# Clearing the buffer of the experts' results: one memset on GpSimd, or eight copies on ScalarE

## The chip, the cores and the metric

The kernel runs on one core of a Trainium2 chip. The metric is device time in microseconds (us) of one execution, as the median of three runs. Engines are called by short names: PE is TensorE (its matmuls; PEld its weight loads), ACT is ScalarE, DVE is VectorE, POOL is GpSimd, SP is the engine that issues most DMAs. Each engine works through its own list of instructions in order; an instruction that waits holds up everything behind it on that engine.

## The reference

Three stages follow each other on 2304 tokens (4 batches of 576).

```python
kv = einsum('bhsd,bhse->bhde', k, v); out = einsum('bhsd,bhde->bhse', q, kv)
x = out / sqrt(mean(out*out) + 1e-6) * g_norm            # attention, 8 heads of 64

logits = x @ w_gate                                      # 8 experts, top 1
e = argmax(logits); gate = softmax(logits)[e]; pos = rank of the token within its expert
h = relu(disp[e] @ w1[e]); y = h @ w2[e]                 # 512 -> 1024 -> 512
out[i] = gate * y[e, pos]                                # if pos < capacity, else 0

a = x @ moe2_w1; b = x @ moe2_w2                         # bilinear stage
out = ((a * b) @ w3) @ w_out
```

## The kernel before, in words

The attention stage takes about the first 75 us; it ends with the gate: for each expert the rows that chose it. The **expert stage** then goes through the eight experts in order of their size (`r` = 0 to 7); expert `r` gets a fixed number of rows `NR[r]` (376, 342, ... 272). Its work is cut into eight steps `m` = 0 to 7, one for each 128 of the 1024 hidden features. In a step PE computes `hp` (`emit_mm1`, L815, 12 matmuls: four pieces of the 512 inputs, three passes each, since every fp32 operand is split into a high part and a low part), ACT writes the high part of `h = relu(hp)` and DVE its low part (`emit_h`, L795 and L799), and two steps later PE multiplies that `h` by the second weight into `yp` (`emit_mm2`, L832, 12 matmuls). So `emit_mm2(r, m - 2)` stands behind `emit_mm1(r, m)` in PE's list, and the low part of h(m-2) must be there by then.

Around these matmuls ACT and DVE have three other jobs in every step, in an order that is written out by hand:

- the expert weights come as pieces of 512 KB (`raw`); ACT writes the high part of a piece (`split_hi`, L731), DVE the low part in two halves (`split_lo`, L740), and then the next piece is loaded
- the weights of the last stage come as 64-bit numbers and are converted in four parts: `conv_a` on ACT (L193, L194), `conv_b` on DVE (L206, L208, L213, L216, L221, L223), `conv_c` on ACT (L239), `conv_d` on DVE (L246). After L213 the next such load is issued; three buffers are in turn
- in steps 4 to 6 the rows of the next expert are transposed (`emit_xt`: PE L764 into `xtp`, ACT L766, DVE L769 and L773); POOL gathered them from DRAM one expert ahead (`emit_gather`, L752) and writes the gates and row numbers to `cmeta` (`emit_meta`, L785)

The results of the experts are copied from PSUM into one buffer in SBUF, `yb` (128 partitions x 4 x 2246 fp32; `emit_y`, L846, L847 and L850, on ACT). Where an expert's columns begin in it is known only at run time, so some columns may not be written by any expert; therefore the whole buffer is cleared once before (L1017, by `POOL.memset`). The first results come into it in step 1 of the second expert.

In the list of POOL the clear stands behind the three gathers of expert 1 and the three `cmeta` writes of expert 0; behind it POOL has nothing before the `cmeta` writes of expert 1. `trir` is a small table of constants whose first row is zeros.

After the experts, nine blocks of 256 rows go through the bilinear stage (L867) and the projection (L884), and the rows are scattered to the output by POOL.

Of the kernel before, what the change touches and what calls it, by code (L numbers as in the profile page):

```python
# [24 lines left out]
def kernel(  # L25
# [39 lines left out]
    PE_, ACT, DVE, POOL, SP = nc.tensor, nc.scalar, nc.vector, nc.gpsimd, nc.sync  # L65
# [5 lines left out]
    YB = sum(NR) - Y0  # L71
    KC = D // 128
# [52 lines left out]
    def ring(name):  # L125
        return ring_p.tile([128, 2, 1024], F32R, tag="ring", name=name)
# [70 lines left out]
    def conv_b():  # L197
        if not stage["b"]:
            return
        c_, raw, x, c = stage["b"].pop(0)  # L200
        if is64:
            TS, STT = DVE.tensor_scalar, DVE.scalar_tensor_tensor
            wh = raw[:, :, 1]
            xi = x.bitcast(I32)
            t = cv_p.tile([128, 512], BF16, tag="t", bufs=1, name="t")
            TS(out=x, in0=x, scalar1=2.0 ** -15, scalar2=122880.0, op0=ALU.max, op1=ALU.min)  # L206
            yield
            TS(  # L208
                out=xi, in0=xi, scalar1=3, scalar2=0x3FFFFFFF,
                op0=ALU.logical_shift_left, op1=ALU.bitwise_and,  # L210
            )
            yield
            STT(out=xi, in0=wh, scalar=-(1 << 30), in1=xi, op0=ALU.bitwise_and, op1=ALU.bitwise_or)  # L213
            load_conv()
            yield
            TS(  # L216
                out=t.bitcast(I16), in0=x.bitcast(I16).rearrange("p (n two) -> p n two", two=2)[:, :, 1],
                scalar1=-128, scalar2=None, op0=ALU.bitwise_and,
            )
            yield  # L220
            DVE.tensor_tensor(out=c, in0=t, in1=c, op=ALU.mult)  # L221
            yield
            DVE.tensor_tensor(out=x, in0=x, in1=c, op=ALU.add)  # L223
        stage["c"].append((c_, x))

    def conv_c():
        if not stage["c"]:
            return
        (what, j, s, _), x = stage["c"].pop(0)
        if what == "u":  # L230
            if is64:
                SP.dma_start(out=ud[j, :, 512 * s:512 * s + 512], in_=x)
            else:
                load_conv()
            return
        if what == "w3" and j not in w3t:
            w3t[j] = ring("w3t")
        t = (wo_t[:, j] if what == "wo" else w3t[j])[:, :, 512 * s:512 * s + 512]
        ACT.copy(t[:, 0], x)  # L239
        stage["d"].append((what, j, x, t))  # L240
# [11 lines left out]
    def weave(*steps):  # L252

        steps = [x for x in steps if x]
        while steps:
            for x in list(steps):
                if next(x, 0) == 0:
                    steps.remove(x)
# [20 lines left out]
    trir = const.tile([128, E, E], F32, name="trir")  # L279
# [445 lines left out]
    def split_hi():  # L725

        i = len(piece)
        if i < NP and raws:
            t = raws.pop(0)
            piece[i] = u7_p.tile([128, 2, 1024], F32R, name="piece") if i == NP - 1 else ring("piece")  # L730
            ACT.copy(piece[i][:, 0, :], t)  # L731
            his.append((piece[i], t))

    def split_lo():

        if his:
            s, t = his.pop(0)
            for h in range(2):
                c = slice(512 * h, 512 * h + 512)
                DVE.tensor_tensor(out=s[:, 1, c], in0=t[:, c], in1=s[:, 0, c].bitcast(F32), op=ALU.subtract)  # L740
                if h == 0:
                    yield
            next_load()
# [14 lines left out]
    def emit_xt(r, j):  # L758
        n = min(128, NR[r] - 128 * j)
        if j == 0:  # L760
            xt[r] = xt_p.tile([128, 2, KC, NR[r]], F32R, tag="xt", name="xt")
        p = one_bank("xtp", [128, KC, 128])
        for c in range(KC):
            PE_.transpose(p[:, c, 0:n], rows[r][0:n, j, 128 * c:128 * c + 128], ident[0:n, 0:n])  # L764
        s = slice(128 * j, 128 * j + n)
        ACT.activation(out=xt[r][:, 0, :, s], in_=p[:, :, 0:n], func=AF.Copy, scale=g2[:, 0:1])  # L766

        def lo():
            DVE.scalar_tensor_tensor(  # L769
                out=xt[r][:, 1, :, s], in0=p[:, :, 0:n], scalar=g2[:, 0:1],  # L770
                in1=xt[r][:, 0, :, s].bitcast(F32), op0=ALU.mult, op1=ALU.subtract,
            )
            DVE.tensor_tensor(  # L773
                out=mt[0:n, r, j, 1:2], in0=rows[r][0:n, j, D:D + 1], in1=keep3[0:n, j:j + 1], op=ALU.mult
            )

        return lo

    def emit_meta(r):
        _, o = nc.values_load_multi_w_load_instructions(  # L780
            rr_i[0:1, 1, r:r + 1], engines=[ET.Pool], min_val=0, max_val=sum(NR[:r])
        )
        for j in range(3):
            n = min(128, NR[r] - 128 * j)
            POOL.dma_start(out=cmeta[ds(o[0] + 128 * j, n), :], in_=mt[0:n, r, j, :])  # L785
# [20 lines left out]
    def emit_mm1(r, m):  # L806
        n = NR[r]
        w = piece[8 * r + 2 * (m // 2)].rearrange("p s (c f) -> p s c f", c=KC)
        p = one_bank("hp")
        i = 0  # L810
        order = [(c, a, b_) for c in range(KC) for a, b_ in PASSES]
        if r == 0 and m == 0:
            order = [(c, a, b_) for a, b_ in PASSES for c in range(KC)]
        for c, a, b_ in order:
            PE_.matmul(  # L815
                p[:, 0:n], lhsT=w[:, a, c, 128 * (m % 2):128 * (m % 2) + 128], rhs=xt[r][:, b_, c, :],
                start=(i == 0), stop=(i == 3 * KC - 1),
            )
            i += 1
        hl[m] = p  # L820
# [128 lines left out]
    with tc.manual_schedule():  # L949
# [48 lines left out]
        yb = y_p.tile([128, KC, YB], F32, name="yb")  # L998
# [15 lines left out]
        rows.pop(0)  # L1014
        emit_gather(1)
        emit_meta(0)
        POOL.memset(yb, 0.0)  # L1017
        split_hi()
        weave(split_lo())
        conv_a()  # L1020
# [4 lines left out]
        for r in range(E):  # L1025
            for m in range(NM):
                i = NM * r + m
                cum += slack[i]
                k = min(len(conv_src), GAP + int((len(conv_src) - GAP) * cum / tot_)) - done
                done += k  # L1030
                ready = [f for f in w3t if w3left[f] == 0]

                xl = None
                if r + 1 < E and m in (4, 5, 6):
                    xl = emit_xt(r + 1, m - 4)
                emit_mm1(r, m)

                bs = [conv_b() for _ in range(min(k, len(stage["b"])))]
                for _ in range(len(stage["c"])):
                    conv_c()  # L1040
                for g in bs:
                    next(g, 0)
                weave(split_lo())
                if xl:
                    xl()
                for g in bs:
                    next(g, 0)
                for _ in range(len(stage["d"])):
                    conv_d()
                for g in bs:  # L1050
                    next(g, 0)
                for f in late:
                    f()
                late = []
                hlo = emit_h(r, m)
                hlo()
                weave(*bs)
                if m >= 2:
                    emit_mm2(r, m - 2)
                elif r:  # L1060
                    emit_mm2(r - 1, NM - 2 + m)
                if m == 1 and r:
                    emit_y(r - 1)
                for f in ready:
                    if f < NG - 1:
                        late.append(emit_w34(f))
                split_hi()
                for _ in range(2 - len(stage["b"])):
                    conv_a()
                if r + 1 < E and m == 7:  # L1070
                    rows.pop(r + 1)
                    emit_meta(r + 1)
                    if r + 2 < E:
                        emit_gather(r + 2)
                if r == E - 1 and m == 3:
                    ACT.copy(ys0[:, 0], yb[:, :, YB - Y0:YB])
                if r == E - 1 and m in (4, 5):
                    c = slice(2 * m - 8, 2 * m - 6)
                    DVE.tensor_tensor(
                        out=ys0[:, 1, c, :], in0=yb[:, c, YB - Y0:YB], in1=ys0[:, 0, c, :].bitcast(F32),  # L1080
                        op=ALU.subtract,
                    )
# [213 lines left out]
```

## Time and profile before

| | us |
|---|---|
| median of three runs | 707.72 |
| the three runs | 713.56, 704.66, 707.72 |
| the profiled execution, its own time | 708.86 |
| its span in the trace | 707.2 |
| PE busy in the span | 644.5 |
| DVE, ACT, POOL busy in the span | 395.4, 295.1, 94.6 |

The profiled execution's time is 1.66 us more than its span in the trace, which runs from the first to the last instruction recorded. In the rows below, "idle before <-releaser" is the time an engine sat idle before an instruction and what ended that. PEclk is the granted TensorE clock, 1.00 for 2.4 GHz and 0.50 for 1.2 GHz.

### The profile page before, as it was taken

How to read it: one execution, taken by the hardware profiler on the slowest of the kernel's cores; microseconds unless marked ns; L12 is line 12 of the kernel's file. 1: busy time of each engine (PE TensorE's matmuls, PEld its weight loads, DVE VectorE, ACT ScalarE, POOL GpSimd, SP SyncE). 2: the span in 40 equal slices, each digit the busy share in tenths (PEclk: the TensorE clock that was granted, in tenths of full speed). 3: DMA queues.
4: the chain of work that ended last, by engine and by line, in shares of the span. 5: the costliest groups of instructions: out<-in, count | busy, mean ns of one | idle time of the engine just before them, and what ended most of it. 6: DMA issues, size and time to landing. Idle time of an engine off the chain costs nothing.

```text
span 707.2 us, 12043 instructions
## 1 busy us (share of the span) xinstructions
PE 644.5 (91%) x4617; PEld 602.9 (85%) x4617; DVE 395.4 (56%) x873; ACT 295.1 (42%) x546; POOL 94.6 (13%) x148
## 2 busy tenths in 40 slices
PE   4976277999999999998999999999999999999993
PEld 3865167998998999998999999999999999999982
DVE  2288879989997988898893753222212121222210
ACT  0545364566655756655663532222222222222210
POOL 3044443202002020202000001010000000000001
PEclk9998569999999999999999999999999999999997
DMA  7991574979899996989774600000000000000000
GB/s 272 349 343 68 196 251 132 174 250 172 308 209 237 242 282 203 267 220 251 237 186 150 163 27 25 7 31 1 31 12 20 16 16 16 16 16 16 16 16 32
DMA packets 35344, 96.78 MB, mean 137 GB/s; under 512 B 8894, under 2 KB 9918, under 8 KB 35282
## 3 DMA queue, kind: packets, MB, share of 16 engines
q1 hardware_dynamic: 28978, 82.48, 39.7%
q0 software_dynamic: 5328, 13.44, 6.5%
q8 instruction: 38, 0.62, 0.4%
q10 hardware_dynamic: 976, 0.04, 0.1%
q14 instruction: 24, 0.20, 0.1%
HBM read 80.15 MB, written 15.79 MB: 136 GB/s over the span
## 4 chain that ended last, share of the span: by engine, by line
issue 41%; PE 28%; DVE 11%; DMA 11%; ACT 4%; POOL 3%; ACTq 0%; POOLq 0%; SPq 0%; DVEq 0%
PE yp L832 9%; PE hp L815 9%; PE w34p L685 5%; DMA w34d<-w34o 4%; POOL out_dram L891 3%; DMA raw<-in_u_dram 2%; PE op L406 2%; DVE x L208 2%; DVE piece L740 1%; DMA raw<-in_w_dram 1%; PE kv L386 1%; ACT piece L731 1%; DMA rows<-xbuf,gidx 1%; PE xtp L764 1%; DMA vin<-in_v_dram 1%
## 5 line engine op out<-in xcount | busy, mean ns | idle before, releaser
L867 PEld LDWEIGHTS ab<-ys,piece 128*128 128x128 f32 x1536 | 186.0, 190 | 1.4
L867 PE MATMUL ab<-ys,piece 128*128 128x256 f32 x1536 | 186.4, 282 | 0.0
L832 PE MATMUL yp<-h,piece 128*128 128x376 f32 (+7 forms) x768 | 123.0, 309 | 9.6 <-DVE h L799 4.9
L815 PE MATMUL hp<-xt,piece 128*128 128x376 f32 (+7 forms) x768 | 124.5, 312 | 2.2 <-ACT xt L766 0.8
L832 PEld LDWEIGHTS yp<-h,piece 128*128 128x128 f32 x768 | 114.4, 190 | 10.9 <-DVE h L799 5.5
L875 DVE TENSOR_TENSOR gt<-at,ab 128x256 f32<-128x256 f32 x64 | 26.9, 420 | 170.5 <-ACT at L873 170.5
L815 PEld LDWEIGHTS hp<-xt,piece 128*128 128x128 f32 x768 | 114.3, 191 | 3.9 <-issue 1.1
L884 PE MATMUL zp<-w,g 128*128 128x512 f32 x432 | 103.8, 396 | 0.0
L740 DVE TENSOR_TENSOR piece<-raw,piece 128x512 fp32r<-128x512 f32 x144 | 92.5, 684 | 14.9 <-ACT piece L731 14.3
L884 PEld LDWEIGHTS zp<-w,g 128*128 128x128 f32 x432 | 80.1, 188 | 18.2
L731 ACT CAST piece<-raw 128x1024 fp32r<-128x1024 f32 x72 | 75.0, 1045 | 2.8 <-DMA raw<-ud 1.6
L873 ACT COPY at<-ab 128x256 f32<-128x256 f32 x64 | 23.8, 372 | 103.1 <-PE ab L867 103.1
L891 POOL DMA_INDIRECT out_dram<-ob,ids x18 | 17.8, 988 | 288.8 <-ACT ob L890 284.1
L877 DVE TENSOR_TENSOR g<-gt,g 128x256 fp32r<-128x256 f32 x72 | 30.6, 426 | 34.0 <-ACT g L876 34.0
L876 ACT CAST g<-gt 128x256 fp32r<-128x256 f32 x72 | 29.3, 407 | 42.9 <-DVE gt L875 42.9
L193 ACT ACTIVATE x<-raw 128x512 f32<-128x512 f32 x40 | 27.1, 678 | 47.6 <-DMA w34d<-w34o 12.9
L685 PE MATMUL w34p<-wo,w3t 128*128 128x512 f32 x192 | 45.3, 391 | 0.0
L890 ACT ACTIVATE ob<-zp,cm 128x512 f32<-128x512 f32 x18 | 12.4, 688 | 76.5 <-PE zp L884 71.5
L685 PEld LDWEIGHTS w34p<-wo,w3t 128*128 128x128 f32 x192 | 35.6, 188 | 7.4 <-DVE xt L769 0.2
L785 POOL DMA_DIRECT2D cmeta<-mt x24 | 13.8, 578 | 209.4 <-DVE mt L773 111.8
L795 ACT ACTIVATE h<-hp 128x376 fp32r<-128x376 f32 (+7 forms) x64 | 27.4, 428 | 28.5 <-PE hp L815 28.5
L799 DVE SCALAR_TENSOR_TENSOR h<-hp,h 128x376 fp32r<-128x376 f32 (+7 forms) x64 | 30.5, 476 | 9.6 <-ACT h L795 9.5
(169 smaller groups left out, 614.7 us busy)
## 6 DMA issues: line engine op xcount, KB each, us to landing
raw<-in_w_dram SPq DMA_DIRECT2D x80, 512.0 KB, 5.7
raw<-in_u_dram SPq DMA_DIRECT2D x16, 512.0 KB, 7.2
qin<-in_q_dram SPq DMA_DIRECT2D x8, 576.0 KB, 6.1
kin<-in_k_dram SPq DMA_DIRECT2D x8, 512.0 KB, 6.5
vin<-in_v_dram SPq DMA_DIRECT2D x8, 512.0 KB, 6.7
raw<-in_w_out_dram SPq DMA_DIRECT2D x8, 512.0 KB, 6.7
ud<-x SPq DMA_DIRECT2D x16, 256.0 KB, 5.3
raw<-ud SPq DMA_DIRECT2D x8, 512.0 KB, 4.5
```

Source lines behind the costliest of these rows:

```text
L685: PE_.matmul(p, lhsT=t[:, a, c, :], rhs=wo_t[:, c // 2, b_, 512 * (c % 2):512 * (c % 2) + 512], start=(i == 0), stop=(i == 3 * NG - 1),)
L731: ACT.copy(piece[i][:, 0, :], t)
L740: DVE.tensor_tensor(out=s[:, 1, c], in0=t[:, c], in1=s[:, 0, c].bitcast(F32), op=ALU.subtract)
L795: ACT.activation(out=t[:, 0, 0:n], in_=p[:, 0:n], func=AF.Relu)
L799: DVE.scalar_tensor_tensor(out=t[:, 1, 0:n], in0=p[:, 0:n], scalar=0.0, in1=t[:, 0, 0:n].bitcast(F32), op0=ALU.max, op1=ALU.subtract,)
L815: PE_.matmul(p[:, 0:n], lhsT=w[:, a, c, 128 * (m % 2):128 * (m % 2) + 128], rhs=xt[r][:, b_, c, :], start=(i == 0), stop=(i == 3 * KC - 1),)
L832: PE_.matmul(yps[r][c // 2][:, c % 2, 0:n], lhsT=w[:, a, m % 2, c, :], rhs=t[:, b_, 0:n], start=(m == 0 and i == 0), stop=(m == NM - 1 and ...
L867: PE_.matmul(p[s][:, 0:n], lhsT=w[:, a, c, 128 * (f % 2):128 * (f % 2) + 128], rhs=y[:, b_, c, 0:n], start=(i == 0), stop=(i == 3 * KC - 1),)
L876: ACT.copy(g[:, 0, f, 0:n], gt)
L877: DVE.tensor_tensor(out=g[:, 1, f, 0:n], in0=gt, in1=g[:, 0, f, 0:n].bitcast(F32), op=ALU.subtract)
L884: PE_.matmul(p, lhsT=g[:, a, f, 128 * t:128 * t + 128], rhs=w34[:, f, b_, :], start=(i == 0), stop=(i == 3 * NG - 1),)
L891: POOL.indirect_dma_start(out=dst, out_offset=bass.IndirectOffsetOnAxis(ap=ids, axis=0), in_=ob, in_offset=None, bounds_check=NT - 1, oob_ ...
```

## The change

The memset on POOL is gone. In its place a list of eight pieces of `yb` is made, each half of one of its four parts (1123 columns in all 128 partitions). In each of the first eight steps of the expert stage (all of them expert 0), right after `split_hi` and ahead of `conv_a`, ACT copies a zero of `trir`, repeated over the piece, into one of them.

```diff
         emit_gather(1)
         emit_meta(0)
-        POOL.memset(yb, 0.0)
+        clear = [(c, h) for c in range(KC) for h in range(2)]
         split_hi()
         weave(split_lo())
         conv_a()
...
                 split_hi()
+                if clear:
+                    c, h = clear.pop(0)
+                    w = yb[:, c, YB // 2 * h:YB // 2 + (YB - YB // 2) * h]
+                    ACT.copy(w, trir[:, 0, 0:1].to_broadcast(list(w.shape)))
                 for _ in range(2 - len(stage["b"])):
                     conv_a()
```

On POOL, at the start of the expert stage (`cmeta<-mt` is `emit_meta(0)`, and what follows is `emit_meta(1)`):

```order
 L785 DMA cmeta<-mt 128x2 x2
 L785 DMA cmeta<-mt 120x2
-L1017 MEMSET yb 128x8984
 L780 TENSOR_LOAD rr_i
 L780 ISA x2
```

One instruction leaves POOL's list there; nothing takes its place.

On ACT, steps 0 to 2 of expert 0 in the changed kernel (`h<-hp` begins the work of a step on `h`, `piece<-raw` is `split_hi`, `x` and `c` are `conv_a`, `wo<-x` is `conv_c`):

```order
L731 CAST piece<-raw 128x1024
L1071 COPY yb<-trir 128x1123
L193 ACTIVATE x<-raw_1076 128x512
L194 ACTIVATE c<-raw_1076 128x512
L239 CAST wo<-x 128x512
L795 ACTIVATE h<-hp 128x376
L731 CAST piece<-raw 128x1024
L1071 COPY yb<-trir 128x1123
L795 ACTIVATE h<-hp 128x376
```

Each of the first eight `piece<-raw` of the steps is now followed by one copy into `yb`; all else on ACT keeps its order, and the lists of PE, DVE and SP are as before.

## Rows read from the trace of the kernel before

**Rows 1.** The page, busy time of each engine over the span.
```profile
PE 644.5 (91%) x4617; PEld 602.9 (85%) x4617; DVE 395.4 (56%) x873; ACT 295.1 (42%) x546; POOL 94.6 (13%) x148
```

**Rows 2.** By stretch: length, busy PE, PEld, DVE, ACT, POOL; PEclk, DMA share, GB/s.
```profile
103.00:113.00 10.00, 5.10 (x29) 4.79 (x28) 9.95 (x4) 1.71 (x3) 8.18 (x3) 0.99 0.36 99
...
180.00:217.00 37.00, 36.39 (x235) 34.63 (x234) 30.90 (x65) 20.49 (x34) 2.92 (x4) 1.00 0.91 246
```

**Rows 3.** Waits of PE, 95 to 400 us: total us, times, longest.
```profile
PE yp L832 <- DVE h L799: 4.9, 1, 4.9
PE yp L832 <- ACT yb L850: 4.7, 3, 2.4
```

**Rows 4.** Timeline of PE: start, us, line, operation, [idle before <-releaser].
```profile
105.43 2.21 PE L815 MATMUL hp<-xt,piece 128*128 128x376 f32 x12
107.48 0.33 PE L832 MATMUL yp<-h,piece 128*128 128x376 f32 x1
112.70 3.71 PE L832 MATMUL yp<-h,piece 128*128 128x376 f32 x11 [4.90 <-DVE h L799]
116.25 0.60 PE L764 MATMUL xtp<-ident,rows 128*128 128x128 f32 x4
```

**Rows 5.** Timeline of DVE, from 102 us, and one instruction of expert 1.
```profile
102.14 9.33 DVE L208 TENSOR_SCALAR x<-x 128x512 int32<-128x512 int32 x1
111.50 0.69 DVE L213 SCALAR_TENSOR_TENSOR x<-raw,x 128x512 int32<-128x512 int32 x1
112.11 0.54 DVE L799 SCALAR_TENSOR_TENSOR h<-hp,h 128x376 fp32r<-128x376 f32 x1
...
139.75 0.69 DVE L206 TENSOR_SCALAR x<-x 128x512 f32<-128x512 f32 x1
```

**Rows 6.** Timeline of POOL, from 101 us, and one gather of expert 2.
```profile
101.83 1.74 POOL L785 DMA_DIRECT2D cmeta<-mt  x3
103.52 7.66 POOL L1017 MEMSET yb<- 128x8984 f32 x1
...
139.10 1.10 POOL L752 DMA_INDIRECT rows<-xbuf,gidx  x1 [0.31 <-issue]
```

**Rows 7.** All instructions of line L208: ns min/median/max.
```profile
L208 DVE TENSOR_SCALAR x<-x x40: 407/419/9327, 84.1 to 363.3; 128x512 int32<-128x512 int32 x40
```

**Rows 8.** PE alone by stretch: length, busy, PEclk, DMA share, GB/s.
```profile
107.80:112.70 4.90, 0.01 (x1) 1.00 0.03 13
112.70:113.70 1.00, 1.00 (x3) 0.53 0.36 74
...
116.70:117.70 1.00, 1.00 (x8) 1.00 0.88 254
```

**Rows 9.** Instructions of ACT by line: busy us, mean ns, idle before.
```profile
L731 ACT CAST piece<-raw 128x1024 fp32r<-128x1024 f32 x72 | 75.0, 1045 | 2.8 <-DMA raw<-ud 1.6 <-DMA raw<-in_w_dram 1.0
...
L239 ACT CAST wo<-x 128x512 fp32r<-128x512 f32 x8 | 4.9, 616 | 13.0 <-DVE x L223 12.9
```

**Rows 10.** ACT alone, expert 0: length, busy, PEclk, DMA share, GB/s.
```profile
99.47:135.00 35.53, 18.80 (x30) 0.95 0.71 182
```

**Rows 11.** Timeline of ACT, step 0 of expert 0, and step 7.
```profile
99.85 1.04 ACT L731 CAST piece<-raw 128x1024 fp32r<-128x1024 f32 x1
100.79 0.68 ACT L193 ACTIVATE x<-raw 128x512 f32<-128x512 f32 x1
101.37 0.69 ACT L194 ACTIVATE c<-raw 128x512 bf16<-128x512 uint32 x1
101.93 0.50 ACT L795 ACTIVATE h<-hp 128x376 fp32r<-128x376 f32 x1
...
132.15 0.49 ACT L795 ACTIVATE h<-hp 128x376 fp32r<-128x376 f32 x1 [2.67 <-PE hp L815]
```

**Rows 12.** The chain that ended last, in order of time: start, us, what.
```profile
143.19 8.05 DMA raw<-in_w_dram
...
192.55 2.04 PE hp L815 x12
```

## The prediction, made before the changed kernel had run

> **What bounds the kernel now.** Begin with the busy times of the page: PE works in 644.5 of 707.2 us, and no other engine comes near that [rows 1]. So a change pays only where PE stands still, or works slowly, for the thing that is changed. The memset is in the expert stage, and there the table by stretch shows one place that is unlike the others: from 103 to 113 us PE is busy for 5.1 of 10 us, against 36.4 of 37 later, and DVE is "busy" for 9.95 us with only four instructions [rows 2]. The waits of PE name what it waits for: once, for 4.9 us, a matmul of L832 waits for the low part of h that DVE writes at L799, the longest single wait of the whole expert stage [rows 3]. The timelines show why. PE finishes `hp` of step 3 at 107.48, issues one matmul of the next group, and the other eleven start at 112.70 [rows 4]. DVE's L799 starts at 112.11, behind L213, which is behind one instruction of L208 that runs from 102.14 for 9.33 us [rows 5]. That line takes 419 ns in the median of 40; this one is the maximum [rows 7]. On POOL the memset of `yb` runs from 103.52 for 7.66 us, to 111.18, and L208 is through 0.29 us later [rows 6]. An elementwise instruction of DVE that lasts 22 times its usual time and ends with the memset is held by the memset; nothing else on the chip ends there.
>
> The stall costs more than the wait. While PE stands, the granted clock is still 1.00; the eleven matmuls behind it run at 0.53 and then 0.50, which is 1.2 GHz, and only by 116.70 it is 1.00 again [rows 8].
>
> **What the removed memset gives back.** Take the group of twelve in which the stall falls. It begins at 107.48, and the next instruction of PE begins at 116.25: 8.77 us. Twelve matmuls of the same size without a stall take 107.48 - 105.43 = 2.05 us [rows 4]. Difference: **6.72 us**, of which 4.90 are the wait and 1.82 the slow clock behind it. Without the wait nothing makes PE idle there, so I take the clock to stay up; should it fall all the same, 4.9 is left.
>
> Does another wait take its place at once? L208 starts at 102.14 as before. At best it takes 0.42 us. At worst POOL's three `cmeta` issues hold it until they are through, 101.83 + 1.74 = 103.57 [rows 6]; in the one other place where such a thing could be seen, a DVE instruction of 0.42 us beside a gather's issue took 0.69 [rows 5, 6], so the truth is nearer the short end, but I reckon with the long one. Then L208 ends at 104.0, L213 (0.69) at 104.7, and h(1) by 105.2. PE wants it from 107.48 on. Cover: 2.3 us.
>
> POOL itself loses nothing and gains nothing: behind the memset it has no work before the `cmeta` writes of expert 1.
>
> **What the eight copies cost.** No row of before shows such a copy: 1123 columns read from one repeated zero in SBUF. The nearest are the casts from SBUF to SBUF, 1045 ns for 1024 columns and 616 ns for 512 [rows 9]: 0.84 ns a column, so 1045 + 99 x 0.84 = **1.13 us**, eight of them 9.0 us. Bounds: below, 1.03, since a cast is followed 0.94 us after its start by the next instruction [rows 11], so 0.1 us overlaps; above, 1.25, since an activation whose input is strided takes 0.68 for 512 columns [rows 11], a tenth more than the 616 ns. A gain from them is excluded: they are added work on an engine that does nothing less.
>
> Is there room on ACT? In the steps of expert 0 it was busy for 18.8 of 35.5 us [rows 10]. The stretch shrinks by 6.7 to 28.8, and 18.8 + 9.0 = 27.8. That is nearly full, so the mean is no comfort, and I walk the list. Step 0: the cast starts at 99.85, 0.94 later the copy, 1.13 later x and c (0.58 and 0.56 apart), so h(1) starts at 101.93 + 1.13 = 103.06 and is done by 103.6. That is before DVE's L213 is through (104.7), so it costs nothing. From h(1) to h(4) ACT has seventeen instructions, with the spacings of [rows 11] 12.0 us, so h(4) is done at 115.0. PE reaches its use in `yp` much later, because `emit_mm2` lags `emit_mm1` by two steps: hp(4) ends at about 112, four groups of 2.05 and two sets of transposes (0.35 each) lie between, so the use is at 121.0. DVE adds about 1.7 us for the low part. Room: 4.3 us. In the same way I get rooms of 2.3 us for h(1), 3.2 for h(2), 4.6 for h(3), 5.9 for h(5); ACT has caught up by step 6, where before it even waited 2.67 us for PE [rows 11]. **Cost on the path: nothing**, covered by that lag of two steps. If the cover went, each 1 us that ACT is late beyond it would be 1 us of PE.
>
> **Behind expert 0.** Everything that PE, ACT and DVE do starts 6.7 us earlier, and loads are issued when an engine frees a buffer, so they move along. The chain of waits shows that from 143 to 192 us the late things are not matmuls but conversions and the transfers in front of them, 8.05 us for one, before it comes back to PE at 192.55 [rows 12]. Each of those links starts when DVE frees a buffer, not at a fixed hour, so the chain moves with the rest. After the experts PE alone sets the pace, with nothing changed.
>
> **Sum.** 6.7 off, 0 added. The profiled execution took 708.86 us (707.2 of span and 1.66 around it): 702.1. The median of the three runs, 707.72, lies 1.1 below it: 701.0. I forecast between the two, **701.5**.
>
> **Rivals.**
>
> *The transfers take it back* (0.17). In the stall the loads nearly stopped too, 0.36 of the DMA engines' time against 0.91 later [rows 2], with buffers full. A PE that runs 6.7 us ahead meets the later transfers of 8 us sooner, and the three waits on `yb`, 4.7 us so far [rows 3], grow. Against it: squeezing 277 us (113 to 390) by 6.7 raises a share of 0.91 only to 0.93. If half is lost: 708.86 - 3.4 = 705.5; if all, 708.9.
>
> *The memset is not what holds L208* (0.06). L208 starts at 102.14, 1.4 us before the memset, and would have been through at 102.6; something held it first [rows 5, 6]. If that something is the `cmeta` issues or a transfer, and lasts, the stall stays and the time is 708.9. Against it stands the end, 0.29 us behind the memset's. The Trainium skill, page "SBUF — State Buffer", section "Who interferes with whom", says that GpSimd and a DVE instruction in a two-port mode exclude each other and that the order of issue decides who blocks: the first one holds the ports to its end. By the starts in the trace L208 came first and POOL should have waited, so by that rule the memset is not the cause and the sum would be 708.9. The ends of both say otherwise, unless POOL's start is recorded late.
>
> *ACT becomes the bound of expert 0* (0.03), the way to **slower**. Place: h(4) to h(7). With copies of d us, h(4) has four of them ahead: PE waits from 4 (d - 1.13) > 4.3, d above 2.2 us. To end behind before, seven copies ahead of h(7) must eat its room of about 6 and the 6.7 gained: 7 (d - 1.13) > 12.7, d above 2.95. At 3.5 us a copy: 7 x 2.37 - 12.7 = 3.9, 712.8. That is three times what the nearest rows say, and nothing else here speaks for it.
>
> *More comes back* (0.04): DVE gets 9.33 - 0.42 = 8.9 us, which could help the conversions that are late from 143 us on: 708.86 - 8.9 = 700.0.
>
> The **forecast** has 0.70.
>
> **Range and chances.** The three runs lie between 704.66 and 713.56, so a median of three moves by 2 to 3 us by itself. From the case with more gain (700.0) less 3 to the half-lost case (705.5) with a little: 697 to 706; left out are the lost cases and the scatter beyond. A difference is told from none at about 2%, 14 us here. No case reaches it; scatter and what I have not thought of get 0.03 for faster and 0.02 for slower, 0.95 is left for the same.
>
> **What would show it.** In the profile after: L208 with a maximum below 2 us; no wait of PE on L799 near 107 us; the clock at 1.00 from 100 us through 125; eight copies of 1.03 to 1.25 us on ACT, and no wait of PE on ACT's h in expert 0; `hp` of expert 1 about 6.7 us earlier, and the first block of the last stage as much earlier. If PE stands at 107 us as before, the second rival is right. If expert 1 starts 6.7 us earlier and the last stage does not, the first one is. A copy above 2 us would undo the reckoning on ACT.

## The result

| | before | after |
|---|---|---|
| median, us | 708.08 | 701.02 |
| lowest and highest, ten runs each | 704.66 to 713.56 | 696.96 to 705.27 |
| profiled execution, us (its span) | 708.86 (707.2) | 698.08 (696.4) |

The changed kernel takes 0.9892 of the time of before, 95% interval 0.9861 to 0.9923: 7.6 us less, with an interval of 5.5 to 9.8. The prediction was 6.7 us less, 701.5.

The profile after. First DVE, at the same place as [rows 5]: L208, L213 and the low part of h(1).

```profile
101.80 0.44 DVE L208 TENSOR_SCALAR x<-x 128x512 int32<-128x512 int32 x1
102.27 0.69 DVE L213 SCALAR_TENSOR_TENSOR x<-raw,x 128x512 int32<-128x512 int32 x1
103.13 0.55 DVE L799 SCALAR_TENSOR_TENSOR h<-hp,h 128x376 fp32r<-128x376 f32 x1 [0.16 <-ACT h L795]
```

L208 takes 0.44 us where it took 9.33, and h(1) is there at 103.7 instead of 112.6. POOL's `cmeta` issues run at the same time:

```profile
101.37 1.74 POOL L785 DMA_DIRECT2D cmeta<-mt  x3
```

The view of all L208 instructions, as in [rows 7], has lost its outlier:

```profile
L208 DVE TENSOR_SCALAR x<-x x40: 406/420/566, 84.3 to 352.3; 128x512 int32<-128x512 int32 x40
```

PE, as in [rows 4]: the twelve matmuls into which the stall fell now run in one piece.

```profile
105.13 2.21 PE L815 MATMUL hp<-xt,piece 128*128 128x376 f32 x12
107.19 2.26 PE L832 MATMUL yp<-h,piece 128*128 128x376 f32 x12
109.28 0.60 PE L764 MATMUL xtp<-ident,rows 128*128 128x128 f32 x4
```

From 107.19 to the next instruction it is 2.09 us, before 8.77. The clock (PE alone by stretch, as in [rows 8]) stays up through the whole stretch and the one in which the matmuls ran at half speed before:

```profile
107.80:112.70 4.90, 4.90 (x32) 1.00 0.76 181
112.70:116.70 4.00, 4.00 (x27) 1.00 0.94 321
```

On ACT, all eight copies (count, ns min/median/max), and ACT's busy time in expert 0 as in [rows 10]:

```profile
L1071 ACT COPY yb<-trir x8: 1126/1137/1158, 100.5 to 126.5; 128x1123 f32<-128x1123 f32 x8
```

```profile
99.47:128.30 28.83, 25.53 (x37) 1.00 0.82 210
```

The waits of PE in the expert stage, from 99 us on, after:

```profile
PE hp L815 <- DVE h L799: 1.1, 1, 1.1
PE yp L832 <- ACT yb L850: 0.9, 1, 0.9
```

Against [rows 3] two things are gone: the 4.9 us of L799, and 3.8 of the 4.7 us on `yb`. The second was not forecast, and the two profiled executions lie 10.8 us apart, more than the medians. The experiments below say which part of that belongs to the change.

Three distances measure this for every run, and the table under the experiments lists them: **expert 0**, from the first matmul of L832 to the first `hp` of expert 1 (128x342); **behind**, from there to the first matmul of L867 in the last stage; and the **rest**, to the end of the span.

### The profile page after: what moved, and what is told of

The parts are those of the page before. It is cut to its first block, busy times and chain, and to the rows that moved or that the text cites. A ratio compares the mean times of both kernels' runs of the same rounds, so it can differ in the third digit from the quotient of the medians.

```text
span 696.4 us, 12049 instructions
## 1 busy us (share of the span) xinstructions
PE 643.1 (92%) x4617; PEld 602.5 (87%) x4617; DVE 387.4 (56%) x873; ACT 303.2 (44%) x554; POOL 88.4 (13%) x147
## 4 chain that ended last, share of the span: by engine, by line
issue 41%; PE 36%; DVE 10%; DMA 6%; POOL 3%; ACT 2%; POOLq 0%; SPq 0%; ACTq 0%; DVEq 0%
PE hp L815 13%; PE yp L832 12%; PE w34p L685 6%; POOL out_dram L891 3%; PE op L406 2%; DMA raw<-in_w_out_dram 1%; DVE piece L740 1%; PE xtp L764 1%; PE kv L386 1%; DMA rows<-xbuf,gidx 1%; DMA vin<-in_v_dram 1%; DVE ssq L417 1%; DMA raw<-in_w_dram 1%; DVE one L561 1%; DMA raw<-ud 1%
## 5 line engine op out<-in xcount | busy, mean ns | idle before, releaser
L867 PEld LDWEIGHTS ab<-ys,piece 128*128 128x128 f32 x1536 | 186.0, 190 | 1.4
L867 PE MATMUL ab<-ys,piece 128*128 128x256 f32 x1536 | 186.4, 282 | 0.0
L815 PE MATMUL hp<-xt,piece 128*128 128x376 f32 (+7 forms) x768 | 124.6, 312 | 2.8 <-DVE h L799 1.1
L832 PE MATMUL yp<-h,piece 128*128 128x376 f32 (+7 forms) x768 | 121.1, 306 | 0.9 <-ACT yb L850 0.9
L815 PEld LDWEIGHTS hp<-xt,piece 128*128 128x128 f32 x768 | 114.5, 191 | 4.2 <-DVE h L799 1.4
L832 PEld LDWEIGHTS yp<-h,piece 128*128 128x128 f32 x768 | 113.1, 188 | 1.7 <-ACT yb L850 1.4
L740 DVE TENSOR_TENSOR piece<-raw,piece 128x512 fp32r<-128x512 f32 x144 | 92.6, 685 | 15.1 <-ACT piece L731 14.4
L799 DVE SCALAR_TENSOR_TENSOR h<-hp,h 128x376 fp32r<-128x376 f32 (+7 forms) x64 | 30.6, 478 | 8.5 <-ACT h L795 8.4
```

The costliest lines, as they stand in the source:

```text
L799: DVE.scalar_tensor_tensor(out=t[:, 1, 0:n], in0=p[:, 0:n], scalar=0.0, in1=t[:, 0, 0:n].bitcast(F32), op0=ALU.max, op1=ALU.subtract,)
L815: PE_.matmul(p[:, 0:n], lhsT=w[:, a, c, 128 * (m % 2):128 * (m % 2) + 128], rhs=xt[r][:, b_, c, :], start=(i == 0), stop=(i == 3 * KC - 1),)
L832: PE_.matmul(yps[r][c // 2][:, c % 2, 0:n], lhsT=w[:, a, m % 2, c, :], rhs=t[:, b_, 0:n], start=(m == 0 and i == 0), stop=(m == NM - 1 and ...
L867: PE_.matmul(p[s][:, 0:n], lhsT=w[:, a, c, 128 * (f % 2):128 * (f % 2) + 128], rhs=y[:, b_, c, 0:n], start=(i == 0), stop=(i == 3 * KC - 1),)
```

## The experiments

The theory: a memset on POOL keeps DVE's tensor_scalar instructions from running; PE then lacks h(1), and falls back to 1.2 GHz; the copies on ACT hide behind the lag of two steps. Tensor_scalar is the kind of DVE instruction that stands at L206, L208 and L216; the expectations call it "two-port". A ratio below is the time of a kernel over that of the kernel before, measured with it, and the brackets hold its 95% interval.

**1. The memset in eight pieces, on POOL, in the same place.**

```diff
-        POOL.memset(yb, 0.0)
+        for c in range(KC):
+            for h in range(2):
+                POOL.memset(yb[:, c, YB // 2 * h:YB // 2 + (YB - YB // 2) * h], 0.0)
```

> The kernel before, with its one memset of 8984 columns on POOL split into eight of 1123 at the same place in POOL's list. Theory (one POOL memset holds a two-port DVE instruction for its whole length, and only for that): L208 is held for one piece at most, some 1.1 us instead of 8.9, h(1) is there by about 104.7 and PE wants it at 107.2, so the wait of 4.9 us is gone and the clock stays at 1.00; ratio to before 0.985 to 0.995, like the change. Rival (POOL keeps DVE out as long as it has such work, however it is cut): L208 or the next two-port instructions lose about 9 us in all, PE waits 4 us or more near 107, ratio 1.00. Rival (the memset does not hold L208 at all): L208 is still 9 us long at 102.

Measured: ratio 1.0015 (0.9982 to 1.0048), no gain at all. The timelines of DVE and POOL, and the view of the eight pieces:

```profile
103.76 9.58 DVE L208 TENSOR_SCALAR x<-x 128x512 int32<-128x512 int32 x1
...
105.11 7.94 POOL L1019 MEMSET yb<- 128x1123 f32 x8
```

```profile
L1019 POOL MEMSET yb<- x8: 1110/1112/1114, 105.1 to 111.9; 128x1123 f32 x8
```

My "for one piece at most" was wrong, the rival right: L208 is held through all eight. The pieces start 0.97 us apart ((111.9 - 105.1) / 7) and last 1.11, so by the record each starts before the last one has ended, with no gap between them in which DVE could begin.

**2. No clearing at all** (the buffer keeps what was in memory where no expert writes).

```diff
-        POOL.memset(yb, 0.0)
```

> The kernel before without any clearing of the buffer (columns that no expert writes keep what was in memory). Theory (the eight copies on ACT are covered): same as the change, ratio to before 0.985 to 0.995, the first matmuls of expert 1 at the same time as with the copies to within 0.3 us. Rival (the copies cost something that the gain hides): expert 1 starts 1 us or more earlier than with the copies, ratio 0.98 or less.

Measured: ratio 0.9898 (0.9865 to 0.9931), and expert 0 takes 24.02 us, with the copies on ACT 24.01. The copies cost nothing on the path.

**3. The whole memset later, at the end of step 3.** A one-column DVE memset makes POOL wait for that point.

```diff
-        POOL.memset(yb, 0.0)
...
+                if r == 0 and m == 3:
+                    DVE.memset(yb[:, 0, 0:1], 0.0)
+                    POOL.memset(yb, 0.0)
                 for _ in range(2 - len(stage["b"])):
```

> The kernel before with the whole memset on POOL moved to the end of step 3 of expert 0 (a one-column DVE memset of 0.1 us, behind L223 of step 3, releases it). There, until step 7, DVE has no tensor_scalar, only tensor_tensor and scalar_tensor_tensor. Theory (only two-port instructions, here L206, L208 and L216, are held by a POOL memset): it runs from about 112 to 121 us beside DVE, no DVE instruction lasts over 1 us, PE does not wait, and the time is that of the change, ratio 0.985 to 0.995, with nothing added to ACT. Rival (a POOL memset holds every DVE instruction): DVE stands for 8 to 9 us from about 112, L740 or L769 is that long, PE waits for about 4 to 5 us, the clock falls again, ratio 1.00.

Measured: ratio 0.9904 (0.9874 to 0.9934), expert 0 in 24.01 us. POOL and what DVE did beside it:

```profile
111.38 7.63 POOL L1069 MEMSET yb<- 128x8984 f32 x1 [8.85 <-DVE yb L1068]
```

```profile
111.73 0.68 DVE L740 TENSOR_TENSOR piece<-raw,piece 128x512 fp32r<-128x512 f32 x1
115.27 0.75 DVE L769 SCALAR_TENSOR_TENSOR xt<-xtp,g,xt 128x512 fp32r<-128x512 f32 x1 [2.85 <-ACT xt L766]
...
116.60 0.54 DVE L799 SCALAR_TENSOR_TENSOR h<-hp,h 128x376 fp32r<-128x376 f32 x1
117.09 1.29 DVE L740 TENSOR_TENSOR piece<-raw,piece 128x512 fp32r<-128x512 f32 x2
```

The same memset, just as long, beside DVE instructions of their usual lengths. No tensor_scalar falls into its time here; in the other traces it holds those, and here it lets tensor_tensor and scalar_tensor_tensor run. So POOL could have kept the work for the price of another place.

**4. The same, released at the end of step 1** (`m == 1` in that edit).

> The same move, but released at the end of step 1, by a one-column DVE memset behind L223 of the first conversion (about 105 us), so that the memset meets L206 and L208 of the next conversion. Theory: L206 at about 107.8 is held until the memset ends at about 113 to 114.4, h(3) is ready at about 116 to 117.3 where PE wants it at 116.3, so PE waits 0 to 1.3 us instead of 4.9: the same hold of 6 us or so costs almost nothing because the room before h(3) is larger than that before h(1); ratio 0.985 to 0.997. Rival (any hold of that length costs PE its 4.9 us): ratio 1.00.

Measured: ratio 0.9922 (0.9889 to 0.9956). DVE, POOL and PE:

```profile
107.16 5.87 DVE L206 TENSOR_SCALAR x<-x 128x512 f32<-128x512 f32 x1
...
105.14 7.62 POOL L1069 MEMSET yb<- 128x8984 f32 x1 [2.00 <-DVE yb L1068]
...
115.81 2.34 PE L815 MATMUL hp<-xt,piece 128*128 128x376 f32 x12 [0.96 <-DVE h L799]
```

Now L206 is held, until 0.27 us after the memset's end. A hold of 5.5 us costs PE 0.96 us here, because h(3), which it delays, is due later than h(1), and the granted clock stays at 1.00 after the pause. The wait is not at the use in `yp`, which I had put at 116.3, but ahead of `hp` of step 5: `hp` and the transposes `xtp` take turns in four PSUM buffers (`one_bank`, `bufs=4`), and `hp` of step 5 takes the one of step 3, which L799 reads until 115.75. Expert 0 takes 25.26 us.

**5. Every copy on ACT three times**, to find where ACT's cover ends.

```diff
-                    ACT.copy(w, trir[:, 0, 0:1].to_broadcast(list(w.shape)))
+                    for _ in range(3):
+                        ACT.copy(w, trir[:, 0, 0:1].to_broadcast(list(w.shape)))
```

> The changed kernel with every copy into the buffer issued three times (24 copies on ACT, three in each step of expert 0). In the trace of the change a copy takes its place on ACT for 1.03 us, so a step's clear now costs 3.1. The prediction's reckoning (h(7) with seven steps ahead, room about 6, gain 6.7) gives 7 x (3.1 - 1.13) - 12.7 = about 1 us more than the kernel before: expert 0 and ACT's lag then decide, PE waits 5 to 14 us on ACT's or DVE's h in expert 0, ratio to before 0.995 to 1.01. By the rooms measured in the trace of the change (3.5 to 6.1 us, and 2.1 us in which ACT only waited for loads) PE waits 4 to 5 us, ratio 0.995 to 0.998. Rival (ACT has slack for any such work, since it is busy for 44% of the span): no wait of PE on h in expert 0, ratio as the change, 0.99.

Measured: ratio 1.007 (1.0041 to 1.0098), slower than before. From the timelines, a step's three copies, PE's longest wait in expert 0 and one in expert 1; then PE alone in a stretch:

```profile
124.05 3.44 ACT L1072 COPY yb<-trir 128x1123 f32<-128x1123 f32 x3
127.40 0.68 ACT L766 ACTIVATE xt<-xtp,g 128x512 fp32r<-128x512 f32 x1
...
117.00 2.33 PE L815 MATMUL hp<-xt,piece 128*128 128x376 f32 x12 [1.87 <-DVE h L799]
...
149.21 1.22 PE L832 MATMUL yp<-h,piece 128*128 128x342 f32 x3 [3.91 <-ACT yb L847]
```

```profile
125.00:130.00 5.00, 5.00 (x17) 0.50 0.65 105
```

Expert 0 takes 32.08 us, 1.4 more than before. The prediction's formula gave 1 with 3.1 us a step; with the 3.35 that three copies took (124.05 to 127.40) it gives 2.8. But the formula has PE waiting for 9.5 us (7 x 2.22 less the room of 6), and in expert 0 PE waits for 4.35: 0.20 for h at L832, and 1.87, 1.77 and 0.51 for one of the four buffers to come free, at L815 (`hp` of step 5), L764 and L815 (step 6). That is in the 4 to 5 of the other figure, whose rooms were reckoned to the use in `yp` only; its ratio was too good, since most of the rest of the 8.07 us over the change is PE at 0.50 of the clock after such waits. So the formula came near in size and not by its mechanism. What both left out is also that ACT's lag goes on into expert 1: the last copies end at 142.5, and the copies of expert 0's results out of PSUM come late, 3.91 us for PE.

**6. The memset ahead of the cmeta issues**, right behind the gathers.

```diff
         emit_gather(1)
+        POOL.memset(yb, 0.0)
         emit_meta(0)
-        POOL.memset(yb, 0.0)
```

> The kernel before with the memset on POOL moved ahead of the three cmeta issues of expert 0 (right behind the gathers of expert 1). Theory (the memset, and not the cmeta issues, holds L208, from the time POOL has it in its queue to its end): POOL's last gather ends about 101.4, the memset runs to about 109.0 and L208 is through 0.2 us after it, 2 us earlier than before; h(1) at 110.3, PE waits about 3 us instead of 4.9; ratio 0.994 to 0.999. Rival (the cmeta issues hold L208): L208 ends when they do, now after the memset, at 111 us as before, wait 4.9, or it is free in 0.4 us because they come late.

Measured: ratio 0.9969 (0.9938 to 1.0). POOL, DVE and PE:

```profile
101.44 7.64 POOL L1016 MEMSET yb<- 128x8984 f32 x1
...
100.20 0.42 DVE L206 TENSOR_SCALAR x<-x 128x512 f32<-128x512 f32 x1
...
101.87 7.49 DVE L208 TENSOR_SCALAR x<-x 128x512 int32<-128x512 int32 x1
...
110.60 3.66 PE L832 MATMUL yp<-h,piece 128*128 128x376 f32 x11 [2.32 <-DVE h L799]
```

L208's end moves 2 us forward with the memset's, and leaves the cmeta issues behind. It is the memset that holds it, as the trace shows; the ratio alone, with an interval that reaches 1.0, would not. L206, which began 1.24 us ahead of the memset, while the last gather ran, was free in 0.42 us, although the memset was next in POOL's list. Expert 0 takes 28.11 us.

**7. Eight pieces on POOL, one in each step**, each released by a one-column DVE memset.

```diff
-                    ACT.copy(w, trir[:, 0, 0:1].to_broadcast(list(w.shape)))
+                    DVE.memset(w[:, 0:1], 0.0)
+                    POOL.memset(w, 0.0)
```

> The clear on POOL in eight pieces as in the second form of the memset, but one piece in each step of expert 0, released by a one-column DVE memset in that step. Theory (pieces back to back overlap, 0.97 us apart and 1.11 long, so the ports were never free between them; with a pause DVE gets in): every two-port DVE instruction waits for one piece at most, 1.1 us, PE does not wait in expert 0, ratio as the change, 0.985 to 0.995. Rival (a POOL memset of any length costs DVE its whole length in the step and the lags add up): L206 or L208 lose 1 us in each of five steps and PE waits 1 us or more.

Measured: ratio 0.9916 (0.9885 to 0.9947), expert 0 in 24.01 us. The one tensor_scalar that met a piece which was running, and one of those that came just ahead of a piece:

```profile
104.80 1.11 DVE L216 TENSOR_SCALAR t<-x 128x512 int16<-128x512 int16 x1
...
109.29 0.42 DVE L206 TENSOR_SCALAR x<-x 128x512 f32<-128x512 f32 x1
...
104.52 1.10 POOL L1072 MEMSET yb<- 128x1123 f32 x1
107.17 1.04 POOL L1072 MEMSET yb<- 128x1123 f32 x1 [1.55 <-DVE yb L1071]
109.44 1.24 POOL L1072 MEMSET yb<- 128x1123 f32 x1 [1.23 <-DVE yb L1071]
```

With pauses between them the pieces are harmless: the worst hold is 0.7 us, in L216. And it goes both ways: L206 began 0.15 us before the third piece and ran its 0.42 us, and the piece took 1.24 instead of 1.04. Two later pieces, at 124.04 and 129.65, each began 0.16 us behind an L206 and took 1.25 and 1.24; the other four took 1.04 and the first 1.10. There is a price elsewhere: POOL's gathers for expert 2 now stand behind the piece of the last step, and PE waits 6.3 us for them in expert 1.

**8. The kernel before again**, for its trace.

> The kernel before once more, for its trace. Theory (what the change's trace gained behind expert 0, 4 us less waiting of PE on yb and on the last experts' rows, is scatter between executions and not the change): the waits of PE from 130 to 400 us on yb and xtp come out differently from the first trace of the same kernel by 2 us or more, while the wait at 107 us is 4.9 again. Rival (they belong to the change): they are 4.7 us on yb and none on xtp again.

Measured, one execution: 711.04 us. Its waits of PE, as in [rows 3]:

```profile
PE yp L832 <- DVE h L799: 4.5, 1, 4.5
PE yp L832 <- ACT yb L850: 3.1, 2, 2.3
PE hp L815 <- DVE h L799: 2.0, 2, 1.1
```

The stall is there again. The waits on `yb` are 3.1 where they were 4.7, and those of `hp` on h are 2.0 where the first trace had 0.6. They differ by 1.6 and 1.4 us, less than the 2 us I had named, so this run alone decides little. The trace of experiment 9, with the stall in it, has 1.8 on `yb` and 5.0 of `hp` on h, and the table below shows the same scatter.

**9 and 10. L208 a little later**, by a DVE memset of 256 or 896 columns ahead of L206 (into a buffer that is overwritten).

```diff
+                if r == 0 and m == 0:
+                    DVE.memset(ys0[:, 0].rearrange("p c n -> p (c n)")[:, 0:256].bitcast(F32), 0.0)
```

> The kernel before with a DVE memset of 256 columns (into a buffer that is written over later) put ahead of L206 of step 0, so that L206 and L208 start about 0.25 us later against POOL's list. What is open: in three traces of the one-piece or back-to-back memset L208 was held though it started 1.26 to 1.38 us before the memset's recorded start. If DVE is shut out whenever POOL has the memset at the head of its waiting work, however late L208 starts, L208 is held again to 0.2 or 0.3 us after the memset, and the time is that of before. If the three were a coincidence of L208 with one of the cmeta issues, L208 may now run in 0.42 to 0.52 us, and then L216, which meets the memset itself, is held instead, with h(1) in time and PE waiting for h(2), about 2 to 3 us near 112, instead of 4.9 near 107.

> The same with 896 columns, so that L206 starts 0.9 us later, close to POOL's cmeta issues and 2 us before the memset, and L208 about 0.4 us before it. If a waiting memset is enough to shut DVE out, L206 may be held already, from 2 us before the memset, and PE waits longer than 4.9 us by up to 1 us; if only a memset that has begun does, L206 and perhaps L208 run in 0.42 us and L216 is held.

Measured, one execution each: 712.18 and 718.04 us. DVE and POOL in the first, then in the second, there with the stall of PE:

```profile
100.79 0.36 DVE L206 TENSOR_SCALAR x<-x 128x512 f32<-128x512 f32 x1
...
102.27 9.19 DVE L208 TENSOR_SCALAR x<-x 128x512 int32<-128x512 int32 x1
103.52 7.66 POOL L1017 MEMSET yb<- 128x8984 f32 x1
```

```profile
102.82 9.95 DVE L206 TENSOR_SCALAR x<-x 128x512 f32<-128x512 f32 x1
103.14 1.74 POOL L785 DMA_DIRECT2D cmeta<-mt  x3
104.82 7.67 POOL L1017 MEMSET yb<- 128x8984 f32 x1
...
115.55 3.82 PE L832 MATMUL yp<-h,piece 128*128 128x376 f32 x11 [6.25 <-DVE h L799]
```

In the second it is L206 that is held, from 2.0 us before the memset's start and 0.3 before the first cmeta issue, and PE waits 6.25 us instead of 4.9. In the first, L206 began 2.7 us ahead and ran free. So a memset that stands in POOL's list behind the `cmeta` issues can hold a tensor_scalar before it begins. Being next in the list is not enough: in experiment 6 it stood behind a gather, and L206 ran free 1.24 us ahead of it. In all six traces with such an early hold (before, 1, 8, 9, 10 and 11) the instruction began during the `cmeta` issues, or in experiment 10 so shortly ahead that its 0.42 us reached into them.

**11. Half on each engine.**

```diff
-        clear = [(c, h) for c in range(KC) for h in range(2)]
+        POOL.memset(yb[:, 2:4], 0.0)
+        clear = [(c, h) for c in range(2) for h in range(2)]
```

> Half and half: POOL clears two of the four parts with one memset of 4492 columns at the old place, ACT the other two with four copies in steps 0 to 3. Theory (the hold is the memset's length and what lies ahead of it, and PE pays what exceeds its room): the memset takes 3.8 us, L208 is held for about 5.4 us, h(1) is ready at about 108.9 where PE wants it at 107.5, PE waits about 1.2 us instead of 4.9 and the clock does not fall for such a short wait; expert 0 up to the first matmul of expert 1 takes about 25.2 us, between 24.0 (the change) and 30.7 (before). Rival (the wait does not depend on the memset's length): 4.9 us and 30.7.

Measured, one execution: 703.99 us; DVE, POOL and PE:

```profile
101.51 5.53 DVE L208 TENSOR_SCALAR x<-x 128x512 int32<-128x512 int32 x1
102.83 3.93 POOL L1017 MEMSET yb<- 128x4492 f32 x1
...
108.28 2.18 PE L832 MATMUL yp<-h,piece 128*128 128x376 f32 x11 [1.07 <-DVE h L799]
```

Half the memset, 1.07 us of waiting, no slow clock: eleven matmuls take 2.18 us, before 3.71. Expert 0 takes 25.34 us, where I expected 25.2.

**The distances**, all from the timelines of PE, in us:

| | expert 0 | behind | rest |
|---|---|---|---|
| before | 30.68 | 252.48 | 320.72 |
| before, again | 30.69 | 251.90 | 321.93 |
| memset in eight, back to back | 30.83 | 254.93 | 321.37 |
| L208 later, 256 | 30.59 | 255.30 | 321.30 |
| L206 held earlier, 896 | 33.08 | 257.02 | 321.49 |
| memset first | 28.11 | 252.32 | 320.88 |
| half on ACT | 25.34 | 253.23 | 321.11 |
| released in step 1 | 25.26 | 250.97 | 321.74 |
| **the change** | 24.01 | 248.40 | 320.96 |
| no clear | 24.02 | 255.70 | 321.81 |
| released in step 3 | 24.01 | 251.67 | 321.69 |
| a piece in each step | 24.01 | 256.22 | 321.45 |
| copies three times | 32.08 | 258.28 | 322.17 |

Expert 0 repeats to a few tenths and orders the kernels as the theory does. Behind, where all rows but the last two do the same work, it lies between 248.4 and 257.0, with or without the stall: no clear has 255.70, the change 248.40. The change's own trace is the lowest of all there, for which nothing in the change accounts.

## Why the prediction was right

**The stall and its size.** Forecast 6.72 us, measured 30.68 - 24.01 = 6.67 in expert 0, the wait and the slow clock both.

**What takes its place.** Nothing, as forecast. I had reckoned with L208 held by the cmeta issues up to 103.6; beside them it took 0.44 us (0.42 to 0.52 in experiments 2, 3 and 4, where no memset stood behind them either). The cover before h(1) was 3.5 us instead of 2.3.

**The copies.** 1.13 us forecast, 1.137 in the median. Walked through by hand, the low part of h(4) was to be ready at 116.7 and wanted at 121.0; in the trace it is ready at 117.4 and wanted at 120.8. ACT had caught up by step 7, a step later than forecast (the 2.67 us quoted for step 6 belong to step 7), and waited 1.21 us for PE there. Before h(4) it also waited 2.1 us for loads, which the walk did not have. Its busy time came to 25.5 us and not 27.8, since instructions that follow at once overlap in the record (a copy takes its place for 1.03 us). Covered altogether: with and without copies expert 0 takes 24.0 us.

The cover is thinner than the walk says, though. It takes the use in `yp` for the due time, but h(4) must have left its PSUM buffer before `hp` of step 6 can begin, as experiments 4 and 5 show. In the trace of the change the low part of h(4) and that `hp` are:

```profile
116.81 0.54 DVE L799 SCALAR_TENSOR_TENSOR h<-hp,h 128x376 fp32r<-128x376 f32 x1
...
118.69 2.31 PE L815 MATMUL hp<-xt,piece 128*128 128x376 f32 x12
```

So the room of h(4) is 1.3 us, where the prediction had 4.3. "Nothing on the path" was right, with a smaller margin than reckoned.

**Behind expert 0.** The shift arrives. Over ten executions of each kernel the change gives 5.5 to 9.8 us, and the first rival, transfers that take it back, would leave 3.4 with half of it lost, which lies outside that. The traces alone could not settle this: behind is 248.4 to 255.7 without the stall (the change, no clear, step 3) and 251.9 to 255.3 with it (before twice, eight pieces, 256). Of the 10.8 us between the two profiled executions 6.67 are expert 0's and 4.1 lie behind, inside that scatter.

**The second rival** is refuted by experiments 3, 4, 6 and 11: L208 or L206 end 0.27 to 0.29 us after the memset, wherever it is put and however long it is. But what spoke for it was real. L208 did begin 1.4 us before the memset. The Trainium skill, page "SBUF — State Buffer", section "Who interferes with whom", lets the instruction that is issued first keep the ports to its end. Experiment 7 agrees: three pieces that met an L206 already running lasted 1.24 or 1.25 us, not 1.04. Experiment 10 does not, if the recorded starts count: L206 began 2.0 us ahead and was held. There the measurement decides. The same section says that tensor_tensor has no two-port mode and contends only with reads of GpSimd; experiment 3 agrees, with L740 at 0.68 us beside the memset.

**The third rival**, ACT as the bound, was near in size: for three copies a step the formula gives 1 to 2.8 us over before in expert 0, and it came to 1.4. That is partly luck: its rooms go by `yp` and not by the PSUM buffers, it has twice the waiting that was measured, and it has neither the slow clock behind the waits nor the lag into expert 1.

**Still open:** what POOL does in the 1.3 to 2.0 us in which a tensor_scalar is held and the memset has not begun. In experiment 7 L208 began 1.28 us before the first piece, beside the same `cmeta` issues, and ran in 0.45. That piece had to wait for the DVE memset ahead of it, but this was through at 101.66, well before L208 began at 103.24. So the `cmeta` issues with a memset behind them are not the whole condition, and I did not find it.

## What to carry to other kernels

In these traces a tensor_scalar of DVE that lasted many times its median, and ended just after a memset on POOL, was being held by that memset; look for the longest maximum in a line of tensor_scalar instructions, not for busy time. It can be cured by moving the work to another engine's slack, by moving it to steps without tensor_scalar, or by pieces with real pauses, but not by pieces that follow each other. What the work then costs on its new engine is read from the due time of what is queued behind it (its use two steps later, or the reuse of its PSUM buffer before that), and not from the engine's busy share.

## What the runs showed that was not expected

- Eight memsets in a row hold a tensor_scalar like one: each starts 0.14 us before the one ahead of it ends.
- A memset behind the `cmeta` issues in POOL's list held a tensor_scalar from up to 2.0 us before its own start.
- `hp` and the transposes share four PSUM buffers, and where ACT or DVE was late PE waited for those more than for h itself.
- The pauses of PE of 2.32 and 4.9 us were followed by matmuls at a granted clock of 0.50 (1.2 GHz), those of 0.96 and 1.07 us by matmuls at 1.00; so 4.9 us of waiting cost 6.7 in expert 0, and 0.96 only 1.25.
- Between executions of kernels that do the same work there, the stage behind expert 0 scatters by 8.6 us (248.4 to 257.0), more than the change is worth. Without the distances by stage, one trace of each kernel would have shown 10.8 us for a change of 6.7.
